# Decode attention beside a feed-forward block on one core: TensorE work regrouped, the output spread to every eighth partition and stored by one DMA

## The chip, the core and the metric

The kernel runs on one core of one Trainium2 chip. The metric is device microseconds of one execution, the median of several runs. Engines are named as in the profile: PE (TensorE, with PEld for its weight loads), DVE (VectorE), ACT (ScalarE), POOL (GpSimd) and SP (SyncE). Sixteen DMA engines move data between the chip's memory and SBUF; an engine that issues a DMA only queues it for them.

## What is computed

One decode step for 4 sequences: a layer norm of x, attention of 32 heads over a cache of 4096 keys and values for each sequence and head, and beside it a feed-forward block with SiLU. Both results are added to x. All tensors are float32.

```python
B, Sq, D = 4, 1, 512;  H, Sk, Dh = 32, 4096, 128;  F = 1792
xn = layernorm(x)
q = (xn @ wq) per head
p = softmax(q . k_cache * Dh ** -0.5)          # over 4096 keys
A = (p . v_cache, heads side by side) @ wo
out = x + A + silu(xn @ w1) @ w2
```

The two caches are 268 MB each, wq and wo 8.4 MB each, w1 and w2 3.7 MB each.

## The kernel before, in words

**Tiles.** The work is cut into T = 32 steps. Step i takes four heads (h to h+3, h = i // 4 * 4) of one sequence (b = i % 4): 8.4 MB of keys and as much of values. A tile has 128 partitions; each head of the four takes 32 of them (PH), and each partition holds 128 keys of 128 numbers. Key tiles have two buffers (kpool), value tiles one (vpool). The weights w1, wq, wo and w2 pass through these same buffers.

**A step.** products (L247, L251): DVE multiplies a quarter of the key tile by the query, which is broadcast in PSUM (q_ps), and POOL adds the two halves of each product row. sums (L262, L263): DVE reduces the rows to scores s. maxima (L267, L269): DVE takes the maximum in each partition and PE transposes the 128 maxima to one row. softmax (L275 to L285): DVE reduces the row to one maximum for each head (gm), PE spreads it to all partitions (L279), ACT scales it (L281) and does four exponentials into p_t, with their sums in l_t. values (L297): 32 matmuls, each of which PE runs as two instructions, multiply p_t with the value tile in four column groups into o_ps; of its rows only a diagonal belongs together. heads_out (L309 to L320): PE sums l_t over each head's partitions (L309), ACT copies o_ps to o_sb (L311), DVE takes the reciprocal (L315) and writes it into the selection weights w_t (L316), and PE adds the diagonal into o_all with four matmuls (L320).

**Order.** All loads go to SP's queue, in the order k of step i+1, then v of step i. A k load waits until its buffer's sums are done, a v load until values has read the one v buffer. The framework orders each engine's instructions by priority and readiness, so an instruction can stand before others that come earlier in the code; on each engine they then run in that order. queries (L232) spreads the four queries of the next heads over the partitions, for four steps at once, into one of two PSUM buffers; in the trace it stands on PE ahead of values.

**Head.** x is normalized by DVE, w1 gives hp (L179), ACT's SiLU follows (L185), PE transposes its result in 112 small instructions (L191), wq gives the queries (L206) which are regrouped (L215 to L223).

**Tail.** After the last step, wo and w2 are loaded in two and four pieces (L359). o_all is copied (L367) and transposed (L370, L375). accumulate (L138) multiplies each of 32 + 14 blocks with its weights: four matmuls of 128 columns each, one to each column group j, into rows 32j to 32j+3 of acc. acc is copied to res (L382), and four DMAs (L385), two from SP and two from ACT, store 4 rows of 128 numbers each. SP waits for them in the program's end (L413).

Of the kernel before, what the change touches and what calls it, by code (L numbers as in the profile page):

```python
# [8 lines left out]
F32 = mybir.dt.float32  # L9
# [14 lines left out]
def kernel(  # L24
# [29 lines left out]
    FC = F // P  # L54
    PH = P // G
# [27 lines left out]
    FJ = F // 4  # L83
    h_sb = scratch[:, 4 * D : 4 * D + FJ]
# [10 lines left out]
    same = const.tile([P, P], F32, name="same")  # L95
    nc.gpsimd.memset(same, 0.0)
    for g in range(G):
        nc.gpsimd.memset(
            same[g * PH : (g + 1) * PH, :].rearrange("p (a g) -> p a g", g=G)[:, :, g], 1.0
        )  # L100
    one = const.tile([1, 1], F32, name="one")
    nc.gpsimd.memset(one, 1.0)
# [3 lines left out]

    W0 = H - G
    w_t = const.tile([P, NR, W0 + H], F32, name="w_t")
# [12 lines left out]
    nc.vector.memset(acc, 0.0)  # L121
    o_all = ps_1.tile([H, B, Dh], F32, name="o_all")
    nc.tensor.matmul(
        o_all.rearrange("h b d -> h (b d)"), w_t[:, 0, :H], p_t.rearrange("p r g -> p (r g)"),
# [8 lines left out]
    )  # L133

    def accumulate(lhsT, rhs, start=False, stop=False):

        for j in range(D // P):
            nc.tensor.matmul(  # L138
                acc[32 * j : 32 * j + B, :], lhsT, rhs[:, j * P : (j + 1) * P],
                start=start, stop=stop,  # L140
            )

    accumulate(ident[:B, :B], x_sb, start=True)
# [32 lines left out]
    hp = ps_s.tile([P, FJ], F32, name="sm")  # L176
    for c in range(DC):
        for j in range(4):
            nc.tensor.matmul(  # L179
                hp[32 * j : 32 * j + B, :], xnT[:, c, :], w1_t[:, c, j * FJ : (j + 1) * FJ],  # L180
                start=(c == 0), stop=(c == DC - 1),
            )
    for j in range(4):
        rows = slice(32 * j, 32 * j + B)
        nc.scalar.activation(h_sb[rows, :], hp[rows, :], AF.Silu)  # L185
    ht_ps = ps_s.tile([P, FC, B], F32, name="sm")
    h_f = h_sb.rearrange("b (m f) -> b f m", f=FC)
    for f in range(FC):
        for j in range(4):
            rows = slice(32 * j, 32 * j + B)  # L190
            nc.tensor.matmul(  # L191
                ht_ps[32 * j : 32 * j + 32, f, :], h_f[rows, f, :], ident[rows, rows],
                start=True, stop=True,
            )
# [223 lines left out]
```

## Time and profile before

| | |
|---|---|
| time, median of 3 runs | 1310.15 us (1309.88 to 1310.94) |
| the profiled execution: its time | 1309.97 us |
| its span, first to last instruction | 1307.9 us |
| bytes moved, mean rate over the span | 561.51 MB, 429 GB/s |
| granted PE clock, mean | 0.646 |

In a row of the timeline stand the start, the duration (us), the engine, the line, the operation, the output and inputs with partitions and elements, the count, and in brackets how long the engine was idle before and what ended that. A row of the groups has the count, the busy time, the mean in ns, and the idle time before. A row of the windows has the stretch, its length, the busy time of PE, PEld, DVE, ACT and POOL with counts, the granted PE clock, the busy share of the 16 DMA engines, and GB/s. A row of the queues has packets, MB and the share of 16 engines' time.

### The profile page before, as it was taken

Reading aid. Unit: us, or ns where it says so; the run is one execution under the profiler, and the core shown is the slowest. Engines: PE = TensorE matmul, PEld = TensorE weight load, DVE = VectorE, ACT = ScalarE, POOL = GpSimd, SP = SyncE. Lnnn points to the kernel's source line nnn. Section 1 sums busy time; section 2 is a strip of 40 time slices with the busy share of each in tenths; the row PEclk is TensorE's granted clock in tenths of the full one; section 3 lists DMA queues with packets and bytes.
Section 4 is the critical chain, followed back from the end, with each engine's and each line's share of the span. In section 5 each row is a group of like instructions: output and inputs, shape, how many; then the busy total and the mean of one; then the engine's idle time right before and its main releaser. Section 6 shows DMA issues by size and latency. Waiting matters only on the chain.

```text
span 1307.9 us, 7983 instructions
## 1 busy us (share of the span) xinstructions
PE 397.9 (30%) x3326; PEld 139.1 (11%) x3326; DVE 911.7 (70%) x439; ACT 97.7 (7%) x329; POOL 511.0 (39%) x144
## 2 busy tenths in 40 slices
PE   3412233320333322133332123332043333113337
PEld 1300011100011100011110001110011111001113
DVE  1499666887666787666687666678666678766660
ACT  1010000000000000000000000000000000000000
POOL 0255333444332444332444433344433344433340
PEclk9656666655666656666665666665566665566669
DMA  9999999999999999999999999999999999999997
GB/s 406 440 425 440 427 437 430 435 435 431 438 427 439 429 436 427 435 433 433 434 429 435 429 437 423 439 429 435 429 423 443 422 443 423 443 421 443 425 427 334
DMA packets 10443, 561.51 MB, mean 429 GB/s; under 512 B 1172, under 2 KB 1188, under 8 KB 1448
## 3 DMA queue, kind: packets, MB, share of 16 engines
q1 hardware_dynamic: 10392, 561.01, 99.4%
q8 instruction: 26, 0.43, 0.1%
q14 instruction: 9, 0.07, 0.0%
q10 hardware_dynamic: 16, 0.00, 0.0%
HBM read 561.00 MB, written 0.01 MB: 429 GB/s over the span
## 4 chain that ended last, share of the span: by engine, by line
DMA 66%; PE 17%; DVE 14%; POOL 3%; issue 0%; SPq 0%; POOLq 0%; DVEq 0%
DMA v_t<-in_A_v_cache_dram 34%; DMA k_t<-in_A_k_cache_dram 29%; PE o_ps L297 15%; DVE k_t L247 9%; DVE s L263 4%; DMA k_t<-in_B_w_dram 3%; POOL k_t L251 3%; PE q_ps L232 1%; DVE s L262 0%; PE sm L269 0%; SPq L359 0%; PE acc L138 0%; DVE gm L275 0%; DVE m L267 0%; SPq L87 0%
## 5 line engine op out<-in xcount | busy, mean ns | idle before, releaser
L251 POOL TENSOR_TENSOR k_t<-k_t 128x2048 f32<-128x2048 f32 (+1 forms) x128 | 508.4, 3983 | 749.5 <-DVE k_t L247 749.5
L247 DVE TENSOR_TENSOR k_t<-k_t,q_ps 128x4096 f32<-128x4096 f32 x128 | 562.4, 4414 | 247.8 <-DMA k_t<-in_A_k_cache_dram 247.8
L297 PE MATMUL o_ps<-v_t,p_t 128*16 128x512 f32 x1984 | 283.2, 735 | 628.7 <-DMA v_t<-in_A_v_cache_dram 624.9
L263 DVE TENSOR_REDUCE s<-k_t 128x32 f32<-128x2048 f32 (+1 forms) x128 | 257.7, 2013 | 11.2 <-POOL k_t L251 11.2
L297 PEld LDWEIGHTS o_ps<-v_t,p_t 128*16 128x16 f32 x1984 | 65.4, 113 | 834.6 <-issue 830.8
L311 ACT ACTIVATE o_sb<-o_ps 128x512 f32<-128x512 f32 x32 | 19.1, 597 | 1081.2 <-PE o_ps L297 1081.2
L262 DVE TENSOR_REDUCE s<-k_t 128x16 f32<-128x2048 f32 x32 | 72.8, 2276 | 0.0
L232 PE MATMUL q_ps<-q_h,ident 32*32 32x512 f32 x64 | 14.0, 974 | 183.2 <-DVE k_t L247 182.5
L285 ACT ACTIVATE p_t<-s,nb 32x128 f32<-32x128 f32 x128 | 66.0, 516 | 2.7 <-ACT nb L281 0.2
L275 DVE TENSOR_REDUCE gm<-sm 1x4 f32<-1x128 f32 x32 | 8.9, 278 | 53.7 <-PE sm L269 53.7
L320 PE MATMUL o_all<-o_sb,w_t 128*32 128x128 f32 x256 | 34.0, 276 | 2.4 <-ACT o_sb L311 0.7
L320 PEld LDWEIGHTS o_all<-o_sb,w_t 128*32 128x32 f32 x256 | 25.8, 110 | 5.4 <-ACT o_sb L311 1.6
L285 ACT ACTIVATION_READ_ACCUMULATOR p_t<-s,nb 32x1 f32 x128 | 25.0, 196 | 0.0
L269 PE MATMUL sm<-ident,m 128*1 128x128 f32 x32 | 8.8, 276 | 42.4 <-DVE m L267 41.9
L232 PEld LDWEIGHTS q_ps<-q_h,ident 32*32 32x32 f32 x64 | 1.6, 128 | 185.7 <-DVE k_t L247 184.1
L279 PE MATMUL sm<-gm,one 1*128 1x4 f32 x64 | 12.5, 264 | 11.9 <-DVE gm L275 11.7
L375 DVE COPY ot<-sm 128x128 f32<-128x128 f32 x1 | 0.3, 292 | 19.3 <-PE sm L370 19.3
L215 DVE COPY q_all<-sm 128x128 f32<-128x128 f32 x1 | 0.3, 292 | 17.6 <-PE sm L206 17.6
L206 PE MATMUL sm<-v_t,xpad 128*32 128x128 f32 x256 | 9.8, 327 | 7.9 <-DMA v_t<-in_A_wq_dram 6.0
L281 ACT ACTIVATE nb<-sm 128x4 f32<-128x4 f32 x32 | 5.6, 174 | 84.7 <-PE sm L279 84.7
L297 PE MATMUL o_ps<-k_t,p_t 128*16 128x512 f32 x64 | 9.4, 753 | 6.6 <-DMA k_t<-in_A_v_cache_dram 6.6
L382 DVE COPY s<-acc 128x128 f32<-128x128 f32 x1 | 0.3, 292 | 15.9 <-PE acc L138 15.9
(66 smaller groups left out, 119.0 us busy)
## 6 DMA issues: line engine op xcount, KB each, us to landing
v_t<-in_A_wo_dram SPq DMA_DIRECT2D x2, 4096.0 KB
k_t<-in_B_w_dram SPq DMA_DIRECT2D x1, 3584.0 KB, 11.5
k_t<-in_B_w_dram SPq DMA_DIRECT2D x1, 1792.0 KB, 33.2
k_t<-in_B_w_dram SPq DMA_DIRECT2D x1, 1024.0 KB, 35.9
k_t<-in_A_k_cache_dram SPq DMA_DIRECT2D x32, 48.3
k_t<-in_B_w_dram SPq DMA_DIRECT2D x1, 512.0 KB, 36.7
v_t<-in_A_v_cache_dram SPq DMA_DIRECT2D x31, 29.4
k_t<-in_B_w_dram SPq DMA_DIRECT2D x1, 256.0 KB, 36.9
```

The costliest lines, as they stand in the source:

```text
L206: nc.tensor.matmul(qp[32 * j : 32 * j + 32, :], xpad[:, c, a : a + PH], wq_t[:, c, h * Dh : (h + 1) * Dh], start=(hl == 0 and c == 0), sto ...
L232: nc.tensor.matmul(t[g * PH : (g + 1) * PH].rearrange("p b d -> p (b d)"), ident[:H, h : h + 1].to_broadcast([H, PH]), q_h.rearrange("h b ...
L247: nc.vector.tensor_tensor(k[:, a:z, :], k[:, a:z, :], q[:, None, :].to_broadcast([P, STEP, Dh]), op=ALU.mult)
L251: nc.gpsimd.tensor_tensor(k[:, a:v, :half], k[:, a:v, :half], k[:, a:v, half:], op=ALU.add)
L262: nc.vector.tensor_reduce(s[:, v:z], k[:, v:z, :], axis=AX, op=ALU.add)
L263: nc.vector.tensor_reduce(s[:, a:v], k[:, a:v, :half], axis=AX, op=ALU.add)
L275: nc.vector.tensor_reduce(gm, mt.rearrange("o (g m) -> o g m", g=G), axis=AX, op=ALU.max)
L279: nc.tensor.matmul(mb, one.to_broadcast([1, P]), gm, start=True, stop=True)
L285: nc.scalar.activation(p_t[rows, :, g], s[rows, :], AF.Exp, bias=nb[rows, g : g + 1], scale=scale, accum_out=l[rows, :],)
L297: nc.tensor.matmul(o[j : j + NR * G, :], p_t[:, rows, :].rearrange("p r g -> p (r g)"), v[:, rows, :].rearrange("p r d -> p (r d)"), start ...
L311: nc.scalar.activation(o_sb.rearrange("p r d -> p (r d)"), o_ps, AF.Copy)
L320: nc.tensor.matmul(o_all[:, b, :], w_t[:, r, W0 - h : W0 - h + H], o_sb[:, r, :], start=False, stop=(i == T - 1 and r == NR - 1),)
```

## The change

The softmax's maximum stays on DVE: it transposes 32x32 blocks, reduces, scales and transposes back, so that each partition has its head's maximum without PE. The exponentials' sums are kept for all steps in l_t and used once, at the end, in place of a reciprocal in each step. heads_out multiplies o_sb by a constant mask (own) and reduces it on DVE, so that one matmul instead of four adds it to o_all. The products of a step are ordered behind the last transpose of the step before, and queries behind values, one step later than before.

In the head, wq is multiplied in matmuls of 512 columns, four heads to each, w1 with strided columns in an order that lets four matmuls transpose the result of the SiLU. In the tail, the blocks of wo and w2's first piece are each one matmul of 512 columns; four blocks share PE's column groups and are summed into part. ACT copies part, and a matmul with the constant fold adds the four rows. Weights for acc have 32 columns with zeros between (OS = 8), so that acc fills all 128 partitions and the result's 16 rows lie in every eighth one. One DMA on SP stores them.

```diff
...
@@ -131,16 +133,29 @@
         ident.rearrange("p (j m) -> p m j", j=4)[:, : NR * G, :],
         axis=AX, op=ALU.add,
     )
+    nc.vector.tensor_reduce(
+        w_t[:, W0 : W0 + G], pick.rearrange("p (r g) -> p g r", r=NR), axis=AX, op=ALU.add
+    )
+    own = const.tile([P, NR], F32, name="own")
+    nc.vector.tensor_reduce(
+        own, pick.rearrange("p (r g) -> p r g", r=NR), axis=AX, op=ALU.add
+    )
+
+
+    OS = PH // B
+    fold = const.tile([P, B, OS], F32, name="fold")
+    nc.gpsimd.memset(fold, 0.0)
+    nc.vector.tensor_copy(fold[:, :, 0], pick[:, :B])
 
     def accumulate(lhsT, rhs, start=False, stop=False):
 
         for j in range(D // P):
             nc.tensor.matmul(
-                acc[32 * j : 32 * j + B, :], lhsT, rhs[:, j * P : (j + 1) * P],
+                acc[PH * j : PH * (j + 1), :], lhsT, rhs[:, j * P : (j + 1) * P],
                 start=start, stop=stop,
             )
 
-    accumulate(ident[:B, :B], x_sb, start=True)
+    accumulate(fold[:B].rearrange("p b s -> p (b s)"), x_sb, start=True)
 
 
     nmean = const.tile([B, 1], F32, name="nmean")
...
-    hp = ps_s.tile([P, FJ], F32, name="sm")
+    hp = ps_s.tile([P, FT * P], F32, name="sm")
+    w1_f = w1_t.rearrange("p c (m f) -> p c f m", f=FC)
     for c in range(DC):
         for j in range(4):
             nc.tensor.matmul(
-                hp[32 * j : 32 * j + B, :], xnT[:, c, :], w1_t[:, c, j * FJ : (j + 1) * FJ],
+                hp[32 * j : 32 * j + B, : FN[j] * P],
+                xnT[:, c, :],
+                w1_f[:, c, F0[j] : F0[j] + FN[j], :],
                 start=(c == 0), stop=(c == DC - 1),
             )
     for j in range(4):
-        rows = slice(32 * j, 32 * j + B)
-        nc.scalar.activation(h_sb[rows, :], hp[rows, :], AF.Silu)
-    ht_ps = ps_s.tile([P, FC, B], F32, name="sm")
-    h_f = h_sb.rearrange("b (m f) -> b f m", f=FC)
-    for f in range(FC):
-        for j in range(4):
-            rows = slice(32 * j, 32 * j + B)
-            nc.tensor.matmul(
-                ht_ps[32 * j : 32 * j + 32, f, :], h_f[rows, f, :], ident[rows, rows],
-                start=True, stop=True,
-            )
-    hT = const.tile([P, FC, B], F32, name="hT")
-    nc.vector.tensor_copy(hT, ht_ps)
-
-
-    HJ = H // 4
-    qp = ps_s.tile([P, Dh], F32, name="sm")
-    for hl in range(HJ):
+        rows, n = slice(32 * j, 32 * j + B), FN[j] * P
+        nc.scalar.activation(h_sb[rows, :n], hp[rows, :n], AF.Silu)
+    ht_ps = ps_s.tile([P, FT, 4, B], F32, name="sm")
+    for t in range(FT):
+        nc.tensor.matmul(
+            ht_ps[:, t],
+            h_sb[:, t * P : (t + 1) * P],
+            ident.rearrange("p (j m) -> p j m", j=4)[:, :, :B],
+            start=True, stop=True,
+        )
+    ht_sb = const.tile([P, FT, 4, B, OS], F32, name="ht_sb")
+    nc.gpsimd.memset(ht_sb, 0.0)
+    nc.vector.tensor_copy(ht_sb[:, :, :, :, 0], ht_ps)
+    hT = [ht_sb[:, t, j] for j in range(4) for t in range(FN[j])]
+
+
+    NM = H // G // 4
+    qp = ps_s.tile([P, G * Dh], F32, name="sm")
+    for m in range(NM):
         for c in range(DC):
             for j in range(4):
-                h = HJ * j + hl
-                a = PH - B - B * hl
+                n = NM * j + m
+                a = PH - B - B * m
                 nc.tensor.matmul(
                     qp[32 * j : 32 * j + 32, :],
                     xpad[:, c, a : a + PH],
-                    wq_t[:, c, h * Dh : (h + 1) * Dh],
-                    start=(hl == 0 and c == 0),
-                    stop=(hl == HJ - 1 and c == DC - 1),
+                    wq_t[:, c, n * G * Dh : (n + 1) * G * Dh],
+                    start=(m == 0 and c == 0),
+                    stop=(m == NM - 1 and c == DC - 1),
                 )
 
-    q_all = const.tile([P, Dh], F32, name="q_all")
-    nc.vector.tensor_copy(q_all, qp)
+
+    q_all = small.tile([P, G, Dh], F32, name="o_sb", bufs=1)
+    nc.vector.tensor_copy(q_all.rearrange("p g d -> p (g d)"), qp)
     qh_ps = ps_q.tile([P, B, Dh], F32, name="q_ps")
     for b in range(B):
-        nc.tensor.matmul(
-            qh_ps[:H, b, :], ident.rearrange("p (h b) -> p b h", b=B)[:, b, :], q_all,
-            start=True, stop=True,
-        )
-    q_h = const.tile([H, B, Dh], F32, name="q_h")
-    nc.vector.tensor_copy(q_h, qh_ps[:H])
-
-    q_ps, vs, st, ls = {}, {}, {}, {}
+        for g in range(G):
+            nc.tensor.matmul(
+                qh_ps[32 * g : 32 * g + 32, b, :],
+                ident.rearrange("p (a b) -> p b a", b=B)[:, b, :],
+                q_all[:, g, :],
+                start=True, stop=True,
+            )
+    q_h = const.tile([P, B, Dh], F32, name="q_h")
+    nc.vector.tensor_copy(q_h, qh_ps)
+
+    q_ps, vs, st = {}, {}, {}
 
     def queries(n):
 
         t = ps_q.tile([P, B, Dh], F32, name="q_ps")
         for g in range(G):
-            h = n * G + g
+            rows = slice(g * PH, (g + 1) * PH)
+            k = g * PH + PH // 4 * (n // NM) + n % NM
             nc.tensor.matmul(
-                t[g * PH : (g + 1) * PH].rearrange("p b d -> p (b d)"),
-                ident[:H, h : h + 1].to_broadcast([H, PH]),
-                q_h.rearrange("h b d -> h (b d)"),
+                t[rows].rearrange("p b d -> p (b d)"),
+                ident[rows, k : k + 1].to_broadcast([PH, PH]),
+                q_h[rows].rearrange("h b d -> h (b d)"),
                 start=True, stop=True,
             )
         for b in range(B):
@@ -263,30 +287,25 @@
         nc.vector.tensor_reduce(s[:, a:v], k[:, a:v, :half], axis=AX, op=ALU.add)
 
     def maxima(i):
-        m = small.tile([P, 1], F32, name="m")
-        nc.vector.tensor_reduce(m, st[i], axis=AX, op=ALU.max)
-        mt = ps_s.tile([1, P], F32, name="sm")
-        nc.tensor.transpose(mt, m, ident)
-        return mt
-
-    def softmax(i, mt):
+
+        nc.vector.tensor_reduce(m_t[:, :1], st[i], axis=AX, op=ALU.max)
+        mt = small.tile([P, PH], F32, name="mt", bufs=1)
+        nc.vector.transpose(mt, m_t)
+        gm = small.tile([P, 1], F32, name="gm", bufs=1)
+        nc.vector.tensor_reduce(gm, mt, axis=AX, op=ALU.max)
+        mb = small.tile([P, PH], F32, name="mb", bufs=1)
+        nc.vector.tensor_scalar_mul(mb, gm.to_broadcast([P, PH]), -scale)
+        nb = small.tile([P, PH], F32, name="nb", bufs=1)
+        return nb, nc.vector.transpose(nb, mb).ins
+
+    def softmax(i, nb):
         s = st.pop(i)
-        gm = small.tile([1, G], F32, name="gm", bufs=1)
-        nc.vector.tensor_reduce(
-            gm, mt.rearrange("o (g m) -> o g m", g=G), axis=AX, op=ALU.max
-        )
-        mb = ps_s.tile([P, G], F32, name="sm")
-        nc.tensor.matmul(mb, one.to_broadcast([1, P]), gm, start=True, stop=True)
-        nb = small.tile([P, G], F32, name="nb", bufs=1)
-        nc.scalar.activation(nb, mb, AF.Copy, scale=-scale)
-        l = small.tile([P, 1], F32, name="l_t")
         for g in range(G):
             rows = slice(g * PH, (g + 1) * PH)
             nc.scalar.activation(
-                p_t[rows, :, g], s[rows, :], AF.Exp, bias=nb[rows, g : g + 1], scale=scale,
-                accum_out=l[rows, :],
-            )
-        ls[i] = l
+                p_t[rows, :, g], s[rows, :], AF.Exp, bias=nb[rows, :1], scale=scale,
+                accum_out=l_t[rows, i % B, i // B, g : g + 1],
+            )
 
     def values(i):
         v, o = vs.pop(i), o_ps
@@ -294,45 +313,45 @@
         for m in range(n):
             j = 32 * (m % 4)
             rows = slice(m * NR, (m + 1) * NR)
-            nc.tensor.matmul(
+            last = nc.tensor.matmul(
                 o[j : j + NR * G, :],
                 p_t[:, rows, :].rearrange("p r g -> p (r g)"),
                 v[:, rows, :].rearrange("p r d -> p (r d)"),
                 start=(m < 4),
                 stop=(m >= n - 4),
             )
+        return last.ins
 
     def heads_out(i):
 
         h, b = i // B * G, i % B
-        lt = ps_s.tile([P, 1], F32, name="sm")
-        nc.tensor.matmul(lt, same, ls.pop(i), start=True, stop=True)
         o_sb = small.tile([P, NR, Dh], F32, name="o_sb", bufs=1)
         nc.scalar.activation(
             o_sb.rearrange("p r d -> p (r d)"), o_ps, AF.Copy
         )
-        rl = small.tile([P, 1], F32, name="rl", bufs=1)
-        nc.vector.reciprocal(rl, lt)
-        nc.vector.tensor_scalar_mul(
-            w_t[:, :, W0 : W0 + G], pick.rearrange("p (r g) -> p r g", r=NR), rl
-        )
-        for r in range(NR):
-            nc.tensor.matmul(
-                o_all[:, b, :], w_t[:, r, W0 - h : W0 - h + H], o_sb[:, r, :],
-                start=False, stop=(i == T - 1 and r == NR - 1),
-            )
+        nc.vector.tensor_tensor(
+            o_sb, o_sb, own[:, :, None].to_broadcast([P, NR, Dh]), op=ALU.mult
+        )
+        o_1 = small.tile([P, Dh], F32, name="o_1", bufs=1)
+        nc.vector.tensor_reduce(o_1, o_sb.rearrange("p r d -> p d r"), axis=AX, op=ALU.add)
+        nc.tensor.matmul(
+            o_all[:, b, :], w_t[:, W0 - h : W0 - h + H], o_1, start=False, stop=(i == T - 1)
+        )
 
     queries(0)
     ks[1] = load_tile(kpool, "k_t", k_cache, 1)
-    mt = None
+    nb = done = None
     for i in range(T):
         if i > 0 and i + 1 < T:
             ks[i + 1] = load_tile(kpool, "k_t", k_cache, i + 1)
-        products(i, 0)
+        with tc.issue_after(done) if i > 0 else nullcontext():
+            products(i, 0)
         if i > 0:
-            softmax(i - 1, mt)
+            softmax(i - 1, nb)
         if i > 0:
-            values(i - 1)
+            with tc.issue_after(values(i - 1)):
+                if i % B == 2 and i + B < T + 2:
+                    queries(i // B + 1)
         if i + 1 < T:
             vs[i] = load_tile(vpool, "v_t", v_cache, i)
         else:
@@ -342,11 +361,9 @@
             sums(i, a - STEP)
         sums(i, R - STEP)
         del ks[i], q_ps[i]
-        mt = maxima(i)
+        nb, done = maxima(i)
         if i > 0:
             heads_out(i - 1)
-        if i % B == 1 and i + B < T:
-            queries(i // B + 1)
 
 
     wo_t = vpool.tile([P, R, Dh], F32, name="v_t").rearrange("p (c m) d -> p c (m d)", c=H)
@@ -358,13 +375,23 @@
         for a, z in zip(edges[:-1], edges[1:]):
             nc.sync.dma_start(t[:, a:z, :], w[:, a:z, :])
 
-    softmax(T - 1, mt)
+    softmax(T - 1, nb)
     values(T - 1)
     heads_out(T - 1)
 
 
+    ls_ps = ps_s.tile([H, B], F32, name="sm")
+    for b in range(B):
+        nc.tensor.matmul(
+            ls_ps[:, b : b + 1], l_t[:, b].rearrange("p n g -> p (n g)"), ones,
+            start=True, stop=True,
+        )
+    rl = const.tile([H, B], F32, name="rl")
+    nc.vector.reciprocal(rl, ls_ps)
     o_row = const.tile([H, B, Dh], F32, name="o_row")
-    nc.scalar.activation(o_row, o_all, AF.Copy)
+    nc.vector.tensor_tensor(
+        o_row, o_all, rl[:, :, None].to_broadcast([H, B, Dh]), op=ALU.mult
+    )
     ot_ps = ps_s.tile([P, B, H], F32, name="sm")
     for n in range(NQ):
         nc.tensor.matmul(
@@ -373,16 +400,25 @@
         )
     ot = const.tile([P, H, B], F32, name="ot")
     nc.vector.tensor_copy(ot, ot_ps.rearrange("p b c -> p c b"))
-    for c in range(H):
-        accumulate(ot[:, c, :], wo_t[:, c, :])
-    for f in range(FC):
-        accumulate(hT[:, f, :], w2_t[:, f, :], stop=(f == FC - 1))
+
+    part = ps_q.tile([P, D], F32, name="q_ps")
+    nc.vector.memset(part, 0.0)
+    rows = [(ot[:, c, :], wo_t[:, c, :]) for c in range(H)]
+    rows += [(hT[f][:, :, 0], w2_t[:, f, :]) for f in range(W2_CUTS[0])]
+    for c, (a, w) in enumerate(rows):
+        j = 32 * (c % 4)
+        nc.tensor.matmul(
+            part[j : j + B, :], a, w, start=(c < 4), stop=(c >= len(rows) - 4)
+        )
+    part_sb = small.tile([P, NR * Dh], F32, name="o_sb", bufs=1)
+    nc.scalar.activation(part_sb, part, AF.Copy)
+    accumulate(fold.rearrange("p b s -> p (b s)"), part_sb)
+    for f in range(W2_CUTS[0], FC):
+        accumulate(hT[f].rearrange("p b s -> p (b s)"), w2_t[:, f, :], stop=(f == FC - 1))
 
     res = small.tile([P, P], F32, name="s")
     nc.vector.tensor_copy(res, acc)
-    for j in range(D // P):
-        eng = nc.sync if j % 2 == 0 else nc.scalar
-        eng.dma_start(of[:, j * P : (j + 1) * P], res[32 * j : 32 * j + B, :])
+    nc.sync.dma_start(of.rearrange("b (j n) -> j b n", j=D // P), res[::OS, :])
```

Left out at the head of the diff: constants that go or come (same and one go; ones, l_t and m_t come, all set on POOL; w_t loses its NR axis), and h_sb, now 512 columns, is set to zero on POOL.

More of the change, by code (lines that the diff above doesn't have):

```diff
@@ L1 @@
-from contextlib import ExitStack
+from contextlib import ExitStack, nullcontext
 import concourse.bass as bass
@@ L54 @@
     FC = F // P
+    FT = 4
+    FN = [(FC + 3 - j) // 4 for j in range(4)]
+    F0 = [sum(FN[:j]) for j in range(4)]
     PH = P // G
@@ L94 @@
     make_identity(nc, ident)
[L95 to L99, printed above, removed]
-        )
-    one = const.tile([1, 1], F32, name="one")
-    nc.gpsimd.memset(one, 1.0)
+    ones = const.tile([P, 1], F32, name="ones")
+    nc.gpsimd.memset(ones, 1.0)
+    nc.gpsimd.memset(h_sb, 0.0)
     nc.vector.memset(xpad, 0.0)
@@ L105 @@
     nc.gpsimd.memset(p_t, 0.0)
+    l_t = const.tile([P, B, H // G, G], F32, name="l_t")
+    nc.gpsimd.memset(l_t, 0.0)
+    m_t = const.tile([P, PH], F32, name="m_t")
+    nc.gpsimd.memset(m_t, 0.0)
     W0 = H - G
-    w_t = const.tile([P, NR, W0 + H], F32, name="w_t")
+    w_t = const.tile([P, W0 + H], F32, name="w_t")
     nc.gpsimd.memset(w_t, 0.0)
```

6 lines of the change are left out of this document (2 added, 4 removed).

## The prediction

> **What bounds the kernel now.** I read the page's busy shares, then its DMA rows and queues.
>
> ```profile
> span 1307.9 us, 7983 instructions
> PE 397.9 (30%) x3326; PEld 139.1 (11%) x3326; DVE 911.7 (70%) x439; ACT 97.7 (7%) x329; POOL 511.0 (39%) x144
> DMA  9999999999999999999999999999999999999997
> q1 hardware_dynamic: 10392, 561.01, 99.4%
> q8 instruction: 26, 0.43, 0.1%
> ```
>
> No engine fills the span: DVE has 70%, PE 30%. The DMA row is at 90% or more in 39 of 40 slices, and the SP queue's packets take 99.4% of 16 engines' time for 561.01 MB, or 429 GB/s. The kernel is a stream of loads with a head and a tail. An edit to an engine matters if it starves the stream, takes bytes out of it, or changes what comes after its last byte.
>
> Does the stream ever run dry? The timeline of two heads in mid-span and of the tightest one answers.
>
> ```profile
> 647.57 0.33 SPq L76 DMA_DIRECT2D v_t<-in_A_v_cache_dram  x1
> 647.94 0.14 DVE L315 RECIPROCAL rl<-sm 128x1 f32<-128x1 f32 x1
> 654.25 8.75 DVE L247 TENSOR_TENSOR k_t<-k_t,q_ps 128x4096 f32<-128x4096 f32 x2 [5.89 <-DMA k_t<-in_A_k_cache_dram]
> 673.72 9.82 PE L297 MATMUL o_ps<-v_t,p_t 128*16 128x512 f32 x64 [24.19 <-DMA v_t<-in_A_v_cache_dram]
> 682.05 0.29 DVE L267 TENSOR_REDUCE m<-s 128x1 f32<-128x128 f32 x1
> 683.60 0.33 SPq L76 DMA_DIRECT2D v_t<-in_A_v_cache_dram  x1
> 692.97 8.76 DVE L247 TENSOR_TENSOR k_t<-k_t,q_ps 128x4096 f32<-128x4096 f32 x2 [8.57 <-DMA k_t<-in_A_k_cache_dram]
> ...
> 948.23 1.93 PE L232 MATMUL q_ps<-q_h,ident 32*32 32x512 f32 x8 [30.44 <-DVE k_t L247]
> 960.04 0.33 SPq L76 DMA_DIRECT2D v_t<-in_A_v_cache_dram  x1
> 964.65 8.75 DVE L247 TENSOR_TENSOR k_t<-k_t,q_ps 128x4096 f32<-128x4096 f32 x2 [3.83 <-DMA k_t<-in_A_k_cache_dram]
> ```
>
> A v load is issued when values (L297) has left the single v buffer; it must be there before the k load ahead of it lands. It is: 6.7 us early at 647.57 (k lands at 654.25), 9.4 at 683.60, 4.6 at 960.04, where the queries matmuls went first. I call this the **cover**. From 654.25 to 692.97 a k and a v tile flow, 16.8 MB in 38.7 us, 433 GB/s: no hole, though the cover differs. So time given back inside the loop is worth nothing; time added costs nothing until it eats the cover.
>
> **The change in the loop.** The rows that price it, from the groups:
>
> ```profile
> L206 PE MATMUL sm<-v_t,xpad 128*32 128x128 f32 x256 | 9.8, 327 | 7.9 <-DMA v_t<-in_A_wq_dram 6.0 <-issue 1.9
> L320 PE MATMUL o_all<-o_sb,w_t 128*32 128x128 f32 x256 | 34.0, 276 | 2.4 <-ACT o_sb L311 0.7
> L309 PE MATMUL sm<-l_t,same 128*128 128x1 f32 x64 | 9.2, 213 | 1.4 <-ACT p_t L285 1.4
> L269 PE MATMUL sm<-ident,m 128*1 128x128 f32 x32 | 8.8, 276 | 42.4 <-DVE m L267 41.9 <-PE o_ps L297 0.3
> L279 PE MATMUL sm<-gm,one 1*128 1x4 f32 x64 | 12.5, 264 | 11.9 <-DVE gm L275 11.7
> L191 PE MATMUL sm<-ident,k_t 4*32 4x4 f32 x112 | 2.8, 200 | 1.5 <-ACT k_t L185 1.5
> L138 PE MATMUL acc<-v_t,ot 128*4 128x128 f32 x256 | 7.4, 273 | 2.7 <-DMA v_t<-in_A_wo_dram 2.3 <-DVE ot L375 0.4
> L138 PE MATMUL acc<-k_t,hT 128*4 128x128 f32 x112 | 4.0, 273 | 2.1 <-DMA k_t<-in_B_w_dram 1.1 <-issue 1.0
> L311 ACT ACTIVATE o_sb<-o_ps 128x512 f32<-128x512 f32 x32 | 19.1, 597 | 1081.2 <-PE o_ps L297 1081.2
> L316 DVE TENSOR_SCALAR w_t<-pick,rl 128x16 f32<-128x16 f32 x32 | 7.5, 234 | 1.1
> L151 DVE TENSOR_TENSOR k_t<-k_t 4x512 f32<-4x512 f32 x1 | 0.7, 680 | 0.0
> L147 DVE TENSOR_REDUCE nmean<-k_t 4x1 f32<-4x512 f32 x1 | 0.7, 673 | 10.3 <-DMA k_t<-in_A_x_dram 10.3
> ```
>
> *PE.* Each matmul shows twice (two passes). L309, L269 and L279 go, L320 falls from 256 to 64, L206 from 256 to 64 wider ones, L191 from 112 to 8, and L138 at the end from 368 to 142 (78 of 512 columns, 8 fold, 56). The query transposes gain 24, the sums of exponentials 8: 842 fewer matmuls of 3326, a quarter, and as many weight loads. PE is 70% idle, so its time is worth nothing here.
>
> *DVE.* Per head L315 (0.14), L316 (0.23) and L275 (a maximum like L267's 0.29, on fewer lanes) go, some 0.7 us. Added are two 32x32 transposes, a maximum and a product on 128x32 (no such transpose in the trace; below 0.29, the larger L267, above nothing, so I take 0.2 each), a multiply like L151 (0.68) and a reduce like L147 (0.67): +1.4 us. The maximum no longer passes through PE. The multiply waits for ACT's copy of o_ps, hence for values: with that copy's 0.6 it ends some 2.1 us after the v issue, when DVE has nothing before the k landing; the shortest such gap is the 4.6 us at 960.04. Hidden. If it ran over, the next product would start that much later and so would a k issue, which has a whole v transfer ahead of it in the stream.
>
> *New waits.* products(i, 0) follows the last transpose on its own engine: nothing else stands behind it. The o_all matmul waits for DVE instead of ACT; behind it on PE is the next values, whose data come 26 us after the v issue. Queries follow values, so the six or so heads like 960.04 get the cover of the others; worth nothing, as the steady 38.7 us shows.
>
> *Head.* The first product waits for data:
>
> ```profile
> 51.80 8.75 DVE L247 TENSOR_TENSOR k_t<-k_t,q_ps 128x4096 f32<-128x4096 f32 x2 [5.25 <-DMA k_t<-in_A_k_cache_dram]
> ```
>
> The wider copies and 24 more small matmuls before it (0.27 each at most, as L320: up to 6 us, or 2 with four column groups at once) fit the 5.25 us or miss by little, and DVE catches up in idle time such as the 8.57 us before 692.97. The POOL memsets have the wait for the weights before them. Nothing.
>
> **The change in the tail.** The timeline of the end, the DMA's last slices, the output's issues and SP's closing semaphores:
>
> ```profile
> 1294.77 3.68 PE L138 MATMUL acc<-v_t,ot 128*4 128x128 f32 x128 [2.31 <-DMA v_t<-in_A_wo_dram]
> 1299.08 1.06 PE L138 MATMUL acc<-k_t,hT 128*4 128x128 f32 x32 [0.63 <-DMA k_t<-in_B_w_dram]
> 1301.17 0.84 PE L138 MATMUL acc<-k_t,hT 128*4 128x128 f32 x24 [1.03 <-issue]
> 1302.21 1.06 PE L138 MATMUL acc<-k_t,hT 128*4 128x128 f32 x32 [0.20 <-DMA k_t<-in_B_w_dram]
> 1303.49 1.05 PE L138 MATMUL acc<-k_t,hT 128*4 128x128 f32 x24 [0.23 <-DMA k_t<-in_B_w_dram]
> 1304.68 0.29 DVE L382 COPY s<-acc 128x128 f32<-128x128 f32 x1 [15.94 <-PE acc L138]
> ```
> ```profile
> 1300.00:1301.00 1.00, 0.14 (x8) 0.00 (x0) 0.00 (x0) 0.00 (x0) 0.00 (x0) 1.00 0.53 215
> 1303.00:1304.00 1.00, 0.77 (x28) 0.32 (x16) 0.00 (x0) 0.00 (x0) 0.00 (x0) 1.00 0.04 16
> ```
> ```profile
> L385 SPq DMA_DIRECT2D out_dram<-s x2: 289/292/295, 1305.0 to 1305.3; - x2
> L385 ACTq DMA_DIRECT2D out_dram<-s x2: 264/439/614, 1305.0 to 1305.7; - x2
> L413 SPq EVENT_SEMAPHORE  x7: 17/28/28, 1306.8 to 1307.9; - x7
> ```
>
> *Store.* The last of four stores is issued at 1305.7 and SP passes its wait at 1306.8, 1.1 us later. One store issued at 1305.0 would be done at 1306.1: 0.7 us saved at most, nothing at least. Its 16 rows make a longer list than 4, so I take **-0.5**. [...]
>
> *Stream end.* The last windows show the 16 DMA engines finishing apart: about half done by 1300, the last piece in only about 3.5 us later. Instruction packets are a load that needn't be even: q8's 0.43 MB is 65 B for each of PE's 6652 instructions, and the change drops 1,684 of them, 0.11 MB. Spread evenly that is 0.11 MB at 429 GB/s, 0.25 us; if the 3.5 us of unevenness is all theirs, a quarter of it gone takes up to 0.9 us. The windows show unevenness, so I take **-0.7**, an estimate.
>
> *PE at the end.* wo in 512-column matmuls, four column groups at once, costs like L297 (64 in 9.82 us or less) against 7.4 before; the later start (about 0.7 us, for DVE's two steps) hides in the 2.31 us wait for wo. After w2's first piece at 1299.08: 14 matmuls (2.1 us by L297), the ACT copy 0.6, fold 0.4, so 1302.2, just when the next piece arrives. The last 24 are as many as before with 32 columns of weights for 4: **+0.1**, bounds 0 and +0.9 if the 1.03 us issue gap recurs there.
>
> Sum: 1309.97 (the profiled execution; 2.07 us outside its span) - 0.5 - 0.7 + 0.1 = 1308.9. The median, 1310.15, stands 0.18 higher: **1309.1**.
>
> **Rivals.**
> - *Nothing comes of it:* completion sets the store, and fetches are even: 1310.15 - 0.25 + 0.1 = 1310.0. For: packet rows name no engine. Against: ACT's late second issue. With it goes the backed-up tail (1309.9 to 1310.9; for: 1302.2 meets 1302.21 without reserve).
> - *The end evens out:* late fetches are what holds the slowest engine, and most of the 3.5 us goes: 1310.15 - 0.7 - 3 = 1306.5. For: PE's own issue gap at 1301 suggests a fetch there. Against: three quarters of the fetches stay.
> - *Slower: values behind DVE.* If DVE's multiply and reduce for one head stood behind all sums of the next head, o_all's matmul and values behind it would wait to 682.3 + 0.9 + 1.35 + 0.3 = 684.9, not start at 673.72; the v issue comes at 694.7, past the k landing at 692.97: a hole of 1.7 us in some 30 heads, 1361. It decides at a delay equal to the cover, 9.4 us. Against: L315, in the same place of the code, runs at 647.94, ahead of L247 at 654.25.
>
> **How the numbers follow.** Forecast 0.60 (own range 1308.2 to 1309.9), nothing or backed up 0.22, evened out 0.10, slower 0.08. The range 1307.4 to 1311.0 leaves the last two out. 0.2% is 2.6 us, about what a measurement can tell from no change: under 1307.5 only the evened end (0.10), over 1312.8 only the late values (0.08), the rest 0.82.
>
> **What would show it.** Right: k landings still 38.7 us apart, q8 near 20 packets, one output issue and SP past its wait about 1.3 us after the copy's end, not 1.8. Wrong: a k landing that comes late with its v issue after it, DVE's multiply behind the next sums, or the DVE copy more than 1.5 us after the last w2 landing.

## The result and the profile after

The changed kernel takes 1308.25 us (median of 22 runs, 1307.87 to 1309.90) against 1310.11 us before (22 runs): ratio 0.9986, 95% interval 0.9980 to 0.9992, 1.9 us less. It lies inside the range, and by 0.05 us inside the forecast's own range, on the faster side of 1309.1.

The page of the changed kernel, its first rows and its queues:

```profile
span 1306.5 us, 6299 instructions
PE 352.5 (27%) x2484; PEld 86.3 (7%) x2484; DVE 974.2 (75%) x540; ACT 92.6 (7%) x297; POOL 511.5 (39%) x144
q1 hardware_dynamic: 10396, 561.01, 99.4%
q8 instruction: 19, 0.31, 0.1%
```

842 matmuls and as many weight loads are gone, and q8, a queue of kind "instruction", carried 19 packets, not 26, each recorded with 16,384 B. I read it as PE's, since its packets follow PE's instructions at about one for 256: 6652 / 26 = 256 before, and at that rate 2 x 2484 = 4968 instructions give 4968 / 256 = 19.4. The loads fill the DMA engines as before (99.4% in both pages).

One step of the loop, in the timeline:

```profile
644.03 0.21 DVE L299 STREAM_TRANSPOSE nb<-mb 128x32 f32<-128x32 f32 x1
644.25 0.33 SPq L80 DMA_DIRECT2D v_t<-in_A_v_cache_dram  x1
644.94 0.69 DVE L332 TENSOR_TENSOR o_sb<-o_sb,own 128x512 f32<-128x512 f32 x1 [0.69 <-ACT o_sb L329]
645.73 1.02 DVE L336 TENSOR_REDUCE o<-o_sb 128x128 f32<-128x512 f32 x1
653.86 8.75 DVE L271 TENSOR_TENSOR k_t<-k_t,q_ps 128x4096 f32<-128x4096 f32 x2 [7.10 <-DMA k_t<-in_A_k_cache_dram]
```

DVE's new work ends 7.1 us before the next keys land. The last key tile, read from the rows of L247 before and L271 after, the last weight loads of PE (PEld) in both, and the tail after:

```profile
1236.59 8.75 DVE L247 TENSOR_TENSOR k_t<-k_t,q_ps 128x4096 f32<-128x4096 f32 x2 [9.02 <-DMA k_t<-in_A_k_cache_dram]
...
1304.14 0.11 PEld L138 LDWEIGHTS acc<-k_t,hT 128*4 128x4 f32 x8 [0.32 <-DMA k_t<-in_B_w_dram]
```
```profile
1236.00 8.75 DVE L271 TENSOR_TENSOR k_t<-k_t,q_ps 128x4096 f32<-128x4096 f32 x2 [7.92 <-DMA k_t<-in_A_k_cache_dram]
...
1298.55 1.90 PE L410 MATMUL q_ps<-k_t,ht_sb 128*4 128x512 f32 x14 [0.75 <-DMA k_t<-in_B_w_dram]
1300.55 0.60 ACT L414 ACTIVATE o_sb<-q_ps 128x512 f32<-128x512 f32 x1 [16.42 <-PE q_ps L410]
1301.20 0.43 PE L153 MATMUL acc<-o_sb,fold 128*32 128x128 f32 x8 [0.76 <-ACT o_sb L414]
1301.45 1.83 PE L153 MATMUL acc<-k_t,ht_sb 128*32 128x128 f32 x56
1302.85 0.16 PEld L153 LDWEIGHTS acc<-k_t,ht_sb 128*32 128x32 f32 x8 [0.18 <-DMA k_t<-in_B_w_dram]
1303.34 0.29 DVE L420 COPY s<-acc 128x128 f32<-128x128 f32 x1 [14.65 <-PE acc L153]
1303.66 0.66 SPq L421 DMA_DIRECT2D out_dram<-s  x1
```

In these two executions the keys' last landing is 0.6 us earlier (1236.59 to 1236.00), w2's first matmul 0.5 us (1299.08 to 1298.55), the last copy 1.3 us (1304.68 to 1303.34), and the end 1.4 us (span 1307.9 to 1306.5). From the copy's end to the span's end it is 2.93 us before and 2.87 after: **the one store saved next to nothing**, though it replaces four. The gain lies ahead of the copy. There the last data come sooner: the last eight weight loads wait for w2's last piece until 1304.14 before and 1302.85 after, 1.3 us earlier, and the copy follows 0.54 and 0.49 us later. So in these two traces the earlier end of the loads is nearly the whole gain. The DMA windows after, beside those of before in the prediction:

```profile
1300.00:1301.00 1.00, 0.45 (x6) 0.00 (x0) 0.00 (x0) 0.45 (x1) 0.00 (x0) 1.00 0.39 154
1302.00:1303.00 1.00, 1.00 (x43) 0.82 (x35) 0.00 (x0) 0.00 (x0) 0.00 (x0) 1.00 0.04 14
1303.00:1304.00 1.00, 0.28 (x8) 0.01 (x1) 0.29 (x1) 0.00 (x0) 0.00 (x0) 1.00 0.00 0
```

The trickle at the end that stood at 0.04 in 1303 to 1304 before (16 GB/s) now stands in 1302 to 1303 (14 GB/s). The medians differ by 1.9 us and the two traced executions by 1.5 (1309.97 and 1308.51 us).

### The profile page after: what moved, and what is told of

The parts are those of the page before. It is cut to its first block, busy times and chain, and to the rows that moved or that the text cites. A ratio compares the mean times of both kernels' runs of the same rounds, so it can differ in the third digit from the quotient of the medians.

```text
span 1306.5 us, 6299 instructions
## 1 busy us (share of the span) xinstructions
PE 352.5 (27%) x2484; PEld 86.3 (7%) x2484; DVE 974.2 (75%) x540; ACT 92.6 (7%) x297; POOL 511.5 (39%) x144
## 3 DMA queue, kind: packets, MB, share of 16 engines
q1 hardware_dynamic: 10396, 561.01, 99.4%
## 4 chain that ended last, share of the span: by engine, by line
DMA 70%; PE 22%; another core or an unknown queue 4%; issue 3%; DVE 0%; ACT 0%; SPq 0%; ACTq 0%
DMA v_t<-in_A_v_cache_dram 66%; PE o_ps L316 21%; DMA k_t<-in_B_w_dram 2%; DMA v_t<-in_A_wq_dram 2%; PE sm L225 1%; PE acc L153 0%; PE q_ps L410 0%; PE q_ps L239 0%; PE q_ps L256 0%; DVE q_h L246 0%; DVE o_sb L235 0%; ACT o_sb L414 0%; ACT o_sb L329 0%; DVE o_sb L332 0%
## 5 line engine op out<-in xcount | busy, mean ns | idle before, releaser
L271 DVE TENSOR_TENSOR k_t<-k_t,q_ps 128x4096 f32<-128x4096 f32 x128 | 562.3, 4414 | 227.9 <-DMA k_t<-in_A_k_cache_dram 227.9
L332 DVE TENSOR_TENSOR o_sb<-o_sb,own 128x512 f32<-128x512 f32 x32 | 21.6, 676 | 26.2 <-ACT o_sb L329 26.0
L337 PE MATMUL o_all<-o,w_t 128*32 128x128 f32 x64 | 15.5, 331 | 89.1 <-DVE o L336 89.1
L336 DVE TENSOR_REDUCE o<-o_sb 128x128 f32<-128x512 f32 x32 | 32.7, 1023 | 3.2
L337 PEld LDWEIGHTS o_all<-o,w_t 128*32 128x32 f32 x64 | 4.9, 118 | 118.4 <-DVE o L336 118.4
L291 DVE TENSOR_REDUCE m_t<-s 128x1 f32<-128x128 f32 x32 | 9.1, 284 | 1.1
L225 PE MATMUL sm<-v_t,xpad 128*32 128x512 f32 x64 | 9.1, 732 | 1.4 <-DMA v_t<-in_A_wq_dram 1.4
L299 DVE STREAM_TRANSPOSE nb<-mb 128x32 f32<-128x32 f32 x32 | 6.8, 212 | 3.3
L410 PE MATMUL q_ps<-v_t,ot 128*4 128x512 f32 x64 | 8.7, 690 | 0.8 <-DMA v_t<-in_A_wo_dram 0.4
L256 PE MATMUL q_ps<-q_h,ident 32*32 32x512 f32 x64 | 8.5, 599 | 0.8 <-DVE q_h L246 0.8
```

Source lines behind the costliest of these rows:

```text
L225: nc.tensor.matmul(qp[32 * j : 32 * j + 32, :], xpad[:, c, a : a + PH], wq_t[:, c, n * G * Dh : (n + 1) * G * Dh], start=(m == 0 and c == ...
L271: nc.vector.tensor_tensor(k[:, a:z, :], k[:, a:z, :], q[:, None, :].to_broadcast([P, STEP, Dh]), op=ALU.mult)
L291: nc.vector.tensor_reduce(m_t[:, :1], st[i], axis=AX, op=ALU.max)
L332: nc.vector.tensor_tensor(o_sb, o_sb, own[:, :, None].to_broadcast([P, NR, Dh]), op=ALU.mult)
L336: nc.vector.tensor_reduce(o_1, o_sb.rearrange("p r d -> p d r"), axis=AX, op=ALU.add)
L337: nc.tensor.matmul(o_all[:, b, :], w_t[:, W0 - h : W0 - h + H], o_1, start=False, stop=(i == T - 1))
```

## Experiments

My theory after the result: PE's instruction packets, fewer now, hold back some DMA engines less. Rivals: the store after all; PE's work in the tail; the loop. Each run is compared with the kernel before on the same chip in five rounds; 0.9986 is 1308.3 us. In the short diffs the changed kernel is the base, but for one, and "..." marks lines left out; the runs with close rows or the old tail also set acc to zero at the start, as the kernel before does.

**The changed kernel again** 

> The changed kernel as it is, timed beside the others of this group so that they can be compared with it on one chip. All theories: 1308.2 us, 0.9986 of the kernel before. Its profile should again show about 19 packets of PE's instruction queue, the k landings 38.7 us apart except for a few gaps that are 0.2 to 1.3 us longer, and SP past its wait 1.8 us after the end of the last copy.

 1308.59 us, ratio 0.9985 (0.9977 to 0.9994), 19 packets. The result repeats; differences below some 0.3 us between kernels mean nothing here.

**Four stores of spread rows**

```diff
-    nc.sync.dma_start(of.rearrange("b (j n) -> j b n", j=D // P), res[::OS, :])
+    for j in range(D // P):
+        eng = nc.sync if j % 2 == 0 else nc.scalar
+        eng.dma_start(of[:, j * P : (j + 1) * P], res[PH * j : PH * (j + 1) : OS, :])
```

> The changed kernel with its one store cut into four of 4 rows each, two from SP and two from ACT, as in the kernel before. Issue theory (the prediction's): the last of four issues starts 0.66 us after the first, so the time rises by 0.5 us to 1308.7. Completion theory (the rival): the write's completion takes its time whatever is issued, and one store of 16 rows takes longer to issue than one of 4, so nothing: 1308.2, with SP past its wait 1.8 us after the copy's end in both.

 1309.66 us, ratio 0.9997 (0.9988 to 1.0006): 1.1 us above the changed kernel, more than either theory said.

```profile
1302.97 0.29 DVE L420 COPY s<-acc 128x128 f32<-128x128 f32 x1 [14.69 <-PE acc L153]
1303.29 1.33 SPq L423 DMA_DIRECT2D out_dram<-s  x2
1303.29 2.17 ACTq L423 DMA_DIRECT2D out_dram<-s  x2
```

Two issues take SP 1.33 us where before two took 0.63. So on SP an issue of 4 rows took 0.66 us with the rows 8 partitions apart and 0.29 (L385 before) with neighbouring rows; one of 16 spread rows also took 0.66 (L421). Spreading the rows made each issue dearer, and joining four into one paid for it.

**Rows close, four stores, all else as changed**

```diff
-    accumulate(fold.rearrange("p b s -> p (b s)"), part_sb)
+    accumulate(pick[:, :B], part_sb)                # and 4-column weights for w2, x
-    nc.sync.dma_start(of.rearrange("b (j n) -> j b n", j=D // P), res[::OS, :])
+    for j in range(D // P):                         # as in the kernel before
```

> The changed kernel with the rows of the result left in partitions 32j to 32j+3, weights of 4 columns, and four stores; all its other matmuls as changed. Theory that a store of rows 8 partitions apart takes 0.66 us to issue, one of neighbouring rows 0.29 (the four spread stores took 1.33 us for two on SP): four close stores end as soon as one spread store, 1308.2 to 1308.5, SP past its wait 1.8 us after the copy. The prediction's theory, that one store saves issues: 0.5 us over the changed kernel, 1308.8.

 1308.36 us, ratio 0.9989 (0.9980 to 0.9998): the changed kernel's time without its spread rows and its one store.

```profile
1303.20 0.63 SPq L424 DMA_DIRECT2D out_dram<-s  x2
1303.21 0.92 ACTq L424 DMA_DIRECT2D out_dram<-s  x2
```

Copy's end to span's end is 2.92 us. The store is settled: neutral.

**The old tail behind the new head and loop**

```diff
-    rows = [(ot[:, c, :], wo_t[:, c, :]) for c in range(H)]
-    ...
+    for c in range(H):
+        accumulate(ot[:, c, :], wo_t[:, c, :])
+    for f in range(FC):
+        accumulate(hT[f][:, :, 0], w2_t[:, f, :], stop=(f == FC - 1))   # and four close stores
```

> The changed kernel with the tail of the kernel before: each of the 32 + 14 blocks multiplied by four matmuls of 128 columns, weights of 4 columns, four stores; the head and the loop stay as changed. It has 452 more PE instructions, all at the end, some 0.03 MB or 2 packets. Fetch theory: these packets come while the last weights flow, and the last landing of w2 comes 0.6 to 1.2 us later for them: 1308.9 to 1309.4. Rival, PE's work in the tail: the last landing stays where it is and the copy starts later behind it. Rival, nothing in the tail mattered: 1308.2.

 1310.08 us (1308.18 to 1311.42), ratio 0.9997 (0.9988 to 1.0006). All the savings in head and loop are there, 21 packets, and the gain in the median is gone, with a wide spread: three of the 11 executions took 1308.2 to 1308.5, the changed kernel's time. The expectation had the last landing late; it isn't. The timeline and the windows:

```profile
1298.00 1.37 PE L154 MATMUL acc<-k_t,ht_sb 128*4 128x128 f32 x41
1301.61 3.82 PE L154 MATMUL acc<-k_t,ht_sb 128*4 128x128 f32 x71 [2.24 <-issue]
1305.48 0.29 DVE L411 COPY s<-acc 128x128 f32<-128x128 f32 x1 [17.08 <-PE acc L154]
```
```profile
1301.50:1302.00 0.50, 0.39 (x12) 0.35 (x16) 0.00 (x0) 0.00 (x0) 0.00 (x0) 0.85 0.09 33
1302.00:1302.50 0.50, 0.50 (x20) 0.40 (x12) 0.00 (x0) 0.00 (x0) 0.00 (x0) 0.50 0.00 0
1302.50:1303.00 0.50, 0.50 (x16) 0.41 (x12) 0.00 (x0) 0.00 (x0) 0.00 (x0) 0.50 0.15 33
```

The data are in by 1302, but PE stood 2.24 us waiting for nothing that the profile shows ("issue"). Just after it went on, its granted clock fell from 1.00 (in 1301 to 1301.5) to 0.50 (from 1302 on), and the last 71 matmuls took 3.82 us, 54 ns each, where the changed kernel's 56 took 33 ns each. At 33 ns they would have ended some 1.5 us sooner (an estimate, 71 times 21 ns). The lone 33 GB/s after the data's end, 16.5 KB in half a microsecond, are an instruction packet: the trace has one of q8 at 1302.6. The packet before it starts at 1299.1, ends at 1300.2, and PE goes on at 1301.6, 1.4 us later. In the kernel before, PE's gap of 1.03 us ends 1.5 us after such a packet (1298.6 to 1299.7, PE at 1301.17). That PE waited for its own instructions is my reading of these two gaps; no row shows it.

**The new tail alone** (base: the kernel before)

```diff
-    for c in range(H):
-        accumulate(ot[:, c, :], wo_t[:, c, :])
-    ...
+    part = ps_q.tile([P, D], F32, name="q_ps")      # and on to the one store, as changed
```

> The kernel before with the changed tail alone: 512-column matmuls into part, the fold, spread rows, one store; head and loop as before. Theory that the tail's PE instructions made the gain (their stalls for instructions and their packets, as the kernel with the old tail suggests): most of the -1.8 us, so 1308.4 to 1309.0. Theory of packets counted over the whole program (the prediction's): 452 of the 1,684 instructions, a quarter of some -0.7, so -0.2, 1309.9. If the loop's part counts besides, the last k landing stays where the kernel before has it, at 1236.6, against 1235.9 with the change.

 1308.37 us, ratio 0.9987 (0.9978 to 0.9995), 24 packets: the whole gain, with the old head and loop. So the savings of loop and head add nothing measurable to the new tail, though they hold 1,232 of the 1,684 instructions saved. The last keys land at 1235.85 here, so the 0.6 us by which they came sooner with the change isn't the loop's doing either. That contradicts a price for each packet, unless it comes in steps.

**53 tiny matmuls in each step**

```diff
                 if i % B == 2 and i + B < T + 2:
                     queries(i // B + 1)
+                more = ps_s.tile([P, B], F32, name="sm")
+                for _ in range(53):
+                    nc.tensor.matmul(
+                        more[:B, :], ident[:, :B], ident[:, :B], start=True, stop=True
+                    )
```

> The changed kernel with 53 more tiny matmuls (4 by 4, into a spare PSUM tile that nothing reads) behind values in each of 31 steps, with queries: 53 x 4 x 31 = 6572 more PE instructions, 0.43 MB or some 26 packets more. Fetch theory with packets on some of the 16 DMA engines: the k landings, which were 3.9 us behind an even beat with 26 packets and 3.1 us with 19, fall behind by some 3 to 4 us more, and the time is 1311 to 1312. Fetch spread evenly: 0.43 MB at 429 GB/s, 1.0 us, 1309.2. Rival, the bytes of instructions don't matter, only PE's work in the tail or in the loop: 1308.2, since the added PE time lies behind the v issue.

 1312.87 us, ratio 1.0020 (1.0012 to 1.0029), 45 packets, last keys at 1239.89: 4.3 us more than the changed kernel. 0.43 MB spread evenly at 429 GB/s would be 1.0 us (an estimate), so it doesn't act as an even load.

**4 wide matmuls in each step**

```diff
+                for _ in range(4):                   # in the place of the 53
+                    nc.tensor.matmul(
+                        more[:B, :], ident[:, :B], q_h.rearrange("h b d -> h (b d)"),
+                        start=True, stop=True,
+                    )
```

> The changed kernel with 4 more matmuls of 512 columns behind values in each of 31 steps, into a spare PSUM tile that nothing reads: PE time like that of the 53 tiny ones (some 7 us each step against 4), but only 496 more instructions, 2 packets. Fetch theory: 0.3 us more than the changed kernel at most, 1308.3 to 1308.7, where the 53 tiny ones gave 1312.9. Rival, added PE time in the loop is what cost there: 1312 or more.

 1308.45 us, ratio 0.9988 (0.9979 to 0.9997), 21 packets. 124 wide matmuls more, some 7 us of PE in each step (an estimate: 4 times the 1.91 us that one of 512 columns, L123, took in the kernel before), leave the time at that of the changed kernel (1308.25 and 1308.59 us). The 1,643 tiny ones of the run before took 2.80 us of PE in a step (at 645.02 in its trace) and 4.3 us in all: in these two runs the number of instructions cost, not PE's time.

**10, 16 and 25 tiny matmuls in each step** (the diff of 53 with another count)

> The changed kernel with 10 of the tiny matmuls behind values in each of 31 steps: 1,240 more PE instructions, so 24 packets of PE's queue where there were 19, as in the kernel with the new tail alone, and none of the added ones in the tail. Linear theory (each packet costs the same: 26 more gave 4.3 us): 5 packets, 0.8 us, 1309.2. Step theory (packets go round 8 DMA engines in turn, as the late k landings of the kernel with 53 suggest, every 8th packet; the stream waits for the engine with the most, 3 for 17 to 24 packets): no change, 1308.3. Tail theory (only what PE fetches in the last 15 us matters): 1308.3.

 1308.34 us, ratio 0.9986 (0.9978 to 0.9995), 24 packets.

> The same with 16 in each step: 1,984 more PE instructions, 27 packets, one more than the kernel before, with the new tail. Linear theory: 8 packets, 1.3 us, 1309.6. Step theory: three engines now have 4 packets, 1.0 to 1.4 us, 1309.3 to 1309.7. Tail theory: 1308.3, though it has more packets than the kernel before; then the gain of the change lies in the tail's instructions alone.

 1309.48 us, ratio 0.9995 (0.9986 to 1.0005), 27 packets.

> The same with 25 in each step: 3,100 more PE instructions, 31 packets. Linear theory: 12 packets, 2.0 us, 1310.3. Step theory: 4 packets on the fullest engine as with 16, so the same time as that kernel, 1309.3 to 1309.7. Tail theory: 1308.3.

 1309.78 us, ratio 0.9997 (0.9988 to 1.0006), 31 packets.

Set beside each other, with the end of the last packet of w2's last piece in each trace:

| packets of q8 | time, us | last load packet ends, us | kernel |
|---|---|---|---|
| 19 | 1308.25, 1308.59, 1308.36 | 1302.35, 1302.18, 1301.88 | changed, again, close rows |
| 20, 21 | 1308.51, 1308.45 | 1301.93, 1301.95 | fold early (below), wide |
| 24 | 1308.34, 1308.37 | 1302.16, 1302.16 | 10 tiny, new tail alone |
| 27 | 1309.48 | 1303.39 | 16 tiny |
| 31 | 1309.78 | 1303.43 | 25 tiny |
| 45 | 1312.87 | 1306.46 | 53 tiny |
| 26 | 1310.11 | 1303.67 | before |

The kernels whose output or old tail costs time of its own are left out, but for the last row. From 19 to 24 the time is flat, from 24 to 27 it jumps 1.1 us, from 27 to 31 it rises 0.3. The end of the loads shows it with less noise: 1302.4 or sooner up to 24 packets, 1303.4 to 1303.7 from 26 to 31. The kernel before stands on the upper step. A line through the end points would put 24 at 1309.1. Steps of 8 fit: packets divided by 8 and rounded up are 3 from 17 to 24, 4 from 25 to 32 and 6 at 45, and the times rise 1.1 us from 3 to 4 and 4.5 from 3 to 6 (1308.34 to 1309.48 and 1312.87). The key landings of the kernel with 16 show the period:

```profile
419.72 8.75 DVE L271 TENSOR_TENSOR k_t<-k_t,q_ps 128x4096 f32<-128x4096 f32 x2 [7.74 <-DMA k_t<-in_A_k_cache_dram]
459.76 8.75 DVE L271 TENSOR_TENSOR k_t<-k_t,q_ps 128x4096 f32<-128x4096 f32 x2 [9.26 <-DMA k_t<-in_A_k_cache_dram]
...
808.29 8.75 DVE L271 TENSOR_TENSOR k_t<-k_t,q_ps 128x4096 f32<-128x4096 f32 x2 [7.47 <-DMA k_t<-in_A_k_cache_dram]
848.32 4.42 DVE L271 TENSOR_TENSOR k_t<-k_t,q_ps 128x4096 f32<-128x4096 f32 x1 [9.24 <-DMA k_t<-in_A_k_cache_dram]
...
1196.86 8.75 DVE L271 TENSOR_TENSOR k_t<-k_t,q_ps 128x4096 f32<-128x4096 f32 x2 [7.19 <-DMA k_t<-in_A_k_cache_dram]
1236.90 4.42 DVE L271 TENSOR_TENSOR k_t<-k_t,q_ps 128x4096 f32<-128x4096 f32 x1 [9.11 <-DMA k_t<-in_A_k_cache_dram]
```

Three intervals are 40.04 us instead of 38.7, 1.33 us late each, and they lie 388.6 us apart. The trace's packet records say which packets these are: the 9th, 17th and 25th of q8 start in them, at 448.1, 839.0 and 1230.0. In the kernel with 53, the five latest landings follow the 9th, 17th, 25th, 33rd and 41st. The durations of the packets repeat with the same period: from the fourth on, those of the kernel with 16 are 1.07, 1.07, 1.07, 1.10, 1.10, 1.10, 1.03 and 1.02 us, then 1.07, 1.07, 1.06, 1.11, 1.10, 1.09, 1.03 and 1.02. So in this trace the keys come 1.33 us late at every eighth packet. In the kernel before, the 25th packet starts at 1298.6, while the last weights flow; with the new tail alone there is no 25th. That the packets go round 8 DMA engines in turn, as the step theory has it, is not shown: no row names an engine.

**Fold early**

```diff
-    rows += [(hT[f][:, :, 0], w2_t[:, f, :]) for f in range(W2_CUTS[0])]
-    for f in range(W2_CUTS[0], FC):
+    for f in range(FC):
```

> The changed kernel with only wo's 32 blocks in part, so that ACT's copy and the fold lie before w2's first piece; all 14 blocks of w2 go to acc in matmuls of 128 columns (168 more PE instructions). Theory that part, copy and fold now back up PE behind w2's first piece: the last matmul ends at the last landing plus 0.3 us, and the time falls by 0.2 to 0.5 us to 1307.9. Rival, the last landing sets the end there: no change, 1308.2; and if the added instructions stall PE at the end as with the old tail, 1309 or more.

 1308.51 us, ratio 0.9986 (0.9978 to 0.9995): no gain. PE runs its 112 matmuls on w2 without a pause, from 1300.18 for 3.24 us, and the last load packet ends at 1301.93, so it is still PE that ends last, with its work moved rather than lifted.

**Four rows, one store: a try for more**

```diff
+    res = small.tile([P, NR * Dh], F32, name="o_sb", bufs=1)      # on close rows
+    for j in range(D // P):                                       # DVE for even j, ACT for odd
+        dst, src = res[:B, j * P : (j + 1) * P], acc[32 * j : 32 * j + B, :]
+        ...                                                       # the copy
+    nc.sync.dma_start(of, res[:B, :])
```

> A try for a faster version: the changed kernel with close rows (weights of 4 columns), acc's four groups copied by DVE and ACT, two each, side by side into 4 rows of 512, and one store of these 4 rows. Theory that the row spacing sets a store's issue (0.29 us for neighbouring rows, 0.66 for every eighth) and that the landing follows 1.0 us after: copies 0.45 us, store 1.3 us, 0.3 us less than the changed kernel, 1308.0. Rival, ACT's copies come late or the store costs as much as the spread one: 1308.3 or more.

 1309.19 us, ratio 0.9993 (0.9984 to 1.0003).

```profile
1303.72 0.28 DVE L425 COPY o_sb<-acc 4x128 f32<-4x128 f32 x1 [13.26 <-PE acc L154]
1304.03 0.27 ACT L427 ACTIVATE o_sb<-acc 4x128 f32<-4x128 f32 x1 [2.43 <-DVE o_sb L425]
1304.33 0.28 DVE L425 COPY o_sb<-acc 4x128 f32<-4x128 f32 x1 [0.34 <-ACT o_sb L427]
1304.65 0.27 ACT L427 ACTIVATE o_sb<-acc 4x128 f32<-4x128 f32 x1 [0.35 <-DVE o_sb L425]
1304.95 0.29 SPq L428 DMA_DIRECT2D out_dram<-o_sb  x1
```

The store did what the theory said: issue 0.29 us, and from the last copy's end to the span's end 2.48 us instead of 2.87. But the copies ran one after the other, 1.2 us instead of 0.29, and lost more. No version here beats the changed kernel.

## Why the prediction was right, and where it was not

- **The stream as the bound, and a loop worth nothing: right.** Landings stayed 38.7 us apart but for the late ones (40.04 in the run with 16). DVE's additions ended 7.1 us before the landing at 653.86; the reduce took 1.02 us, not 0.67, and was hidden all the same. It reads with a stride and writes 128 columns, not one; no run says which of the two makes it dearer. The new tail alone gave the whole gain. That the loop's instructions were worth nothing beside it holds because the tail's 452 alone get below 25 packets.
- **Store, -0.5: wrong; about -0.1 measured** (2.93 to 2.87 us). The failed step is "Its 16 rows make a longer list than 4", which looked at the count of rows. Their spacing made the issue dear: 0.66 us spread, 0.29 close, both on SP. The sign "about 1.3 us after the copy's end, not 1.8" failed too: SP passed its wait at 1305.4, 1.8 us after the copy's end, as before. With a cheap issue (four rows, 0.29 us) SP waited 1.0 us after it, 1.3 us from the issue's start.
- **Stream end, -0.7: right in its cause, wrong in its form.** More PE instructions did hold back the stream, by far more than their packets' bytes: the 26 packets more of the run with 53 cost 4.3 us, their 0.43 MB would take 1.0 us at 429 GB/s. But "a quarter of it gone takes up to 0.9 us" priced them in proportion. In these runs they cost in steps that fit 8 packets: from 27 down to 24 gives 1.1 us in the medians (1309.48 to 1308.34), from 26 to 19, the change's own step, 1.3 in the traced end of the loads (1303.67 to 1302.35), and the five packets from 24 to 19 nothing (1308.34 to 1308.25). The prediction had no step, so that the change crossed one was luck.
- **PE at the end, +0.1: about right for the change; what the old tail can cost was not priced.** The chain part, copy, fold came out as worked (1.90, 0.60, 0.43) and meets the last landing; in the second trace of the changed kernel it ends later than the data, and the copy comes at 1303.63 instead of 1303.34. The old tail's 368 pairs of a short matmul and its weight load had PE standing 2.24 us in the old-tail run's profile; the data were in by 1302 (DMA share 0.00 in 1302 to 1302.5), a clock of 0.50 followed, and PE ended last. In the kernel before the gap was 1.03 us, and PE still waited for data at 1304.14, so there it cost nothing in the traced execution. Its medians leave 0.2 to 0.5 us for it (1310.01 us on the chip where 25 and 16 tiny matmuls with the new tail took 1309.78 and 1309.48). What decides how long PE stands stays open.
- **The sum: inside the range, in part by luck.** It forecast -1.1 us and -1.9 came. The store was counted 0.4 too high and the end of the stream 0.4 to 0.6 too low, and these errors partly cancel. Of the 1.9 us, the traced pair shows 1.3 as the earlier end of the loads and some 0.1 as the store. The rest, some 0.5 us, is not traced; the old tail may hold 0.2 to 0.5 of it.
- **Rivals.** "The end evens out" (1306.5) did not happen, and unevenness stays: the DMA share is 0.39 in 1300 to 1301. "Nothing comes of it" was right about the store alone. The backed-up tail shows in the second trace, where it is worth 0.3 us. Values never fell behind DVE: L332 runs at 644.94, ahead of L271 at 653.86.

## What to carry to other kernels

In this kernel, bound by its loads, PE's idle time hid its work (124 wide matmuls more: 1308.45 us) but not its instructions: with about one packet of q8 for 256 of them, the loads ended at 1302.16 us with 24 packets, 1303.39 with 27 and 1306.46 with 45, in steps. So count packets before and after a change. At the end, where the last data meet the last arithmetic, try few wide matmuls in place of many short ones: with the old tail's 368 short ones PE stood 2.24 us in the profile. Before joining stores, look at what one issue costs for the layout that joining needs: here 0.66 us on SP for spread rows, 0.29 for close ones.

## What the runs showed of the hardware beyond that

- 6,572 added PE instructions, 26 packets or 0.43 MB of q8, cost 4.3 us (1308.59 to 1312.87) in a stream that moves 0.43 MB in 1.0 us at its 429 GB/s.
- With the old tail, PE's granted clock fell to 0.50 just after a 2.24 us gap (1302 to 1305), and its matmuls then ran 54 ns apart (71 in 3.82 us), where 41 before the gap took 1.37 us, 33 ns each.
- In the changed kernel's trace a DVE transpose of 128x32 float32 in 32x32 blocks took 0.21 us (L299), a reduce of 128x512 to 128x128 with a stride 1.02 us (L336).
